# Dealing one burst of an attention kernel out over three units of its main loop

## The chip, the cores and the metric

The kernel runs on one core of one Trainium2 chip. The metric is the device time of one execution in microseconds (us). It is compared as a median over runs. Engines are named as in the profile: PE is the matrix engine (PEld its weight loads), DVE the vector engine, ACT the engine of the activations, POOL is GpSimd, SP the engine that only issues DMAs here.

## The reference

Attention whose scores are masked by a hash of six sign bits, and then a feed-forward stage with the maximum of three projections:

```python
def _attn_ref(q, k, v, proj):              # q, k, v: 4 x 8 heads x 768 x 64; proj: 64 x 6
    ...
    q_bits = (np.einsum('bhsd,dk->bhsk', q, proj) > 0).astype(np.int64)
    k_bits = (np.einsum('bhsd,dk->bhsk', k, proj) > 0).astype(np.int64)
    q_bucket = np.sum(q_bits * powers, axis=-1)
    k_bucket = np.sum(k_bits * powers, axis=-1)
    mask = q_bucket[:, :, :, None] == k_bucket[:, :, None, :]
    scores = scale * np.matmul(q, k.transpose(0, 1, 3, 2))
    scores = np.where(mask, scores, -1000000000.0)
    ...
    attn = np.exp(scores)
    attn = attn / (np.sum(attn, axis=-1, keepdims=True) + 1e-09)
    return np.matmul(attn, v).astype(np.float32)

def _moe_ref(x, w1, w2, w3, w_out):        # x: 3072 x 512; w1, w2, w3: 512 x 768; w_out: 768 x 512
    h = np.maximum(np.maximum(x @ w1, x @ w2), x @ w3)
    return (h @ w_out).astype(np.float32)
```

The output of the attention, with the heads side by side, is the `x` of the second function.

## The kernel before

**Units.** The main loop (L607 to L632) runs over 192 units, 48 to a batch (`UPB`). A unit is two blocks of 128 keys against 384 queries of one head: two score matmuls into one PSUM tile `sc` (L290, the sign bits ride along as extra rows of `S`), and one exponential on ACT (L292), which writes a weights tile `AT` of 128 x 768. There are 26 such tiles, used in turn. Six units make a group: the keys of two heads against one half of the queries.

**What a unit issues, in order.** Each engine works through its own queue in the order in which the program is written; no scheduler moves anything. A unit `u` issues: the scores of unit `u + 1` (before unit 35, of `u + 2`); whatever the table `at` holds for it (loads, `turn`, `narrow`, `place`); one piece of the feed-forward stage, if one is due (from unit 40 on, `ffn_at`); `gather(u)`; the entries of `firsts` for it; and, in some units, a `burst`.

**gather (L334 to L344).** From unit 36 on, DVE adds up the weights tiles of a group in `As` (L342, L344), so that fewer matmuls are needed for the sums. The first unit of three issues nothing.

**Values, sums, scaling (`quads`, L347 to L389).** Two groups make a quad. `values` (L317) runs 24 matmuls, 32 columns of the array each, four side by side, into a PSUM tile `av`; each quad needs two, w = 0 and w = 1. `sums` (L367) runs, for weights not added up before, another 24 matmuls of that kind into `sm`; then DVE makes the inverses: a transpose (`ys`, L326), an addition and a reciprocal (`rr`, L327 and L328). `scale` transposes the inverses back (`rb`, L374, once for both w), takes a small column (`sv`, L377) and writes one slice of `xT`, the input of the feed-forward stage (L386). The feed-forward matmuls of L405 read four slices of `xT` in turn, for the output piece `l`.

**Where the quads stand.** The first two quads of the first batch are dealt out by `quad_at`: sums, first values with their scaling, and second values with their scaling, each in a unit of its own (units 18, 20, 23 and 26, 29, 32). The third quad, groups 4 and 5, is a `burst` in unit 36: values, sums, values, and both scalings behind them. It fills the third and fourth slices of the first `xT`. In unit 40 the feed-forward stage begins to read that `xT`. The fourth quad of the batch is a burst in unit 48, and after that a burst of two quads comes every 24 units.

**PSUM.** From unit 34 on (`LAST`) the scores have two tiles `sc` (`s0`, `s1`), `av` has `m0`, and everything else takes `m1`, `m2`, `m3` in turn (L613).

**Inputs of the second batch.** `turn` (L197, DVE) transposes the loaded `nat` tile into `T32`, four pieces to a set. `narrow` (L202, POOL) turns that into bf16, `place` (L208, SP) moves it into `S` by DMA, and `quad_hash` (L218 on PE, L221 on DVE, L228 on SP) adds the sign bits. For one set the four turns stand in units 34 to 37.

Of the kernel before, what the change touches and what calls it, by code (L numbers as in the profile page):

```python
# [17 lines left out]
def kernel(  # L18
# [59 lines left out]
    def lay_out(**tags):  # L78
        rings.update(tags)
        if "pool" in rings:  # L80
            third.close()
        rings["pool"] = third.enter_context(tc.tile_pool(name="third_ps", bufs=1, space=bass.MemoryType.PSUM))
# [128 lines left out]
    def quad_hash(g):  # L211
        bp = ps_tile("bp")
        ts = [t32.pop((side, g)) for side in range(2)]
        for u in range(2):
            for side in range(2):
                for j in range(2):
                    r = 2 * side + j
                    nc.tensor.matmul(bp[Q * r : Q * (r + 1), 0:HALF], pj[:, u, :],  # L218
                                     ts[side][:, u, j * HALF : (j + 1) * HALF], start=(u == 0), stop=(u == 1))
        bits = b_pool.tile([P, HALF], BF16, tag="bits", name="bits")  # L220
        nc.vector.tensor_scalar(out=bits[:], in0=bp[:, 0:HALF], scalar1=0.0, scalar2=0.5,  # L221
                                op0=AluOp.is_gt, op1=AluOp.subtract)

        def send():
            for side in (1, 0):
                for j in range(2):
                    r = 2 * side + j
                    nc.sync.dma_start(s_of[side, g][D : D + KB, :, j * HALF : (j + 1) * HALF],  # L228
                                      bits[Q * r : Q * (r + 1), :])
        return send  # L230
# [34 lines left out]
    UPB = NU // B  # L265
# [3 lines left out]
    def unit_of(u):  # L269
        g, n = divmod(u, UPG)  # L270
        if g < 4:
            hd, n = divmod(u % (2 * UPG), UPG)
            return 2 * (g // 2) + n // MH, hd, n % MH
        return g, n // MH, n % MH
# [6 lines left out]
    def scores(u):  # L281
        g, hd, kp = unit_of(u)
        b, qh, jj = groups[g]
        hh = b * H + 2 * jj + hd
        (qn, qx), (kn, kx) = where[0, hh], where[1, hh]
        nb = NBITS if b == 0 else KB
        sc = ps_tile("sc", "sc")
        for j in range(2):
            m = 2 * kp + j
            nc.tensor.matmul(sc[:, j, 0:HALF], s_of[kn][0 : D + nb, kx, m * P : (m + 1) * P],  # L290
                             s_of[qn][0 : D + nb, qx, qh * HALF : (qh + 1) * HALF], start=True, stop=True)
        nc.scalar.activation(at_tiles[u % NAT][:, :, 0:HALF], sc[:, :, 0:HALF], ActFn.Exp,  # L292
                             bias=-SCALE * 0.25 * nb, scale=SCALE)
# [40 lines left out]
    def gather(u):  # L334
        g, hd, kp = unit_of(u)
        if u < 36 or kp == 0:
            return
        if kp == 1:
            as_of[g, hd] = as_pool.tile([P, 2, HALF], FP16, tag="as", name="As")
        t, new = as_of[g, hd], at_tiles[u % NAT][:, :, 0:HALF]  # L340
        old = at_tiles[(u - 1) % NAT][:, :, 0:HALF] if kp == 1 else t[:]
        nc.vector.tensor_tensor(out=t[:], in0=old, in1=new, op=AluOp.add)  # L342
        if kp == 2 and u >= 48:
            nc.vector.tensor_tensor(out=t[:, 0, :], in0=t[:, 0, :], in1=t[:, 1, :], op=AluOp.add)  # L344
# [103 lines left out]
    def when(u, f, *args):  # L448
        at.setdefault(u, []).append(lambda: f(*args))

    with tc.manual_schedule():
# [121 lines left out]
        def hash_due(u):  # L573
            if u in hash_at:
                when(u + 1, quad_hash(hash_at[u]))


        def burst(u, *gss):
            vals, sums, scale = quads(gss)
            every = [(i, w) for i in range(len(gss)) for w in range(2)]  # L580
            ahead = 2 if u == NU else 1
            for n, (i, w) in enumerate(every):
                if n == ahead:
                    sums()
                    hash_due(u)
                vals(i, w)
                if n == ahead:
                    for e in every[:ahead]:
                        scale(*e)
                if n >= ahead:  # L590
                    scale(i, w)


        firsts = {}

        def quad_at(gs, us, ua, ub):
            vals, sums, scale = quads([gs])
            for u, fs in ((us, [sums]), (ua, [lambda: vals(0, 0), lambda: scale(0, 0)]),
                          (ub, [lambda: vals(0, 1), lambda: scale(0, 1)])):
                firsts.setdefault(u, []).extend(fs)  # L600

        quad_at((0, 1), *[18, 20, 23])
        quad_at((2, 3), *[26, 29, 32])
        firsts.setdefault(32, []).append(lambda: hash_due(32))

        issued, MORE, LAST = 0, 11, 3 * UPB // 4
        for u in range(NU):  # L607
            while issued < min(u + 2 if MORE - 2 <= u < LAST - 1 else u + 1, NU - 1):
                issued += 1
                if issued == MORE:  # L610
                    lay_out(sc=['s2', 's0', 's1'], ms=['m0', 'm1'])
                if issued == LAST:
                    lay_out(sc=['s0', 's1'], ms=["m1", "m2", "m3"], av=["m0"])  # L613
                scores(issued)
            for f in at.pop(u, []):
                f()
            if u in ffn_at:
                ffn += ffn_groups(ffn_at[u])
            full = u % 24 == 23
            if full:  # L620
                gather(u)
            if ffn:
                ffn.pop(0)()
            if not full:
                gather(u)
            w = u - LAG
            for f in firsts.pop(u, []):
                f()
            if UPB // 2 <= w < UPB and w % 12 == 11:
                burst(u, [w // 6 - 1, w // 6])  # L630
            elif w >= UPB and w % 24 == 23:
                burst(u, [w // 6 - 3, w // 6 - 2], [w // 6 - 1, w // 6])  # L632
# [39 lines left out]
```

## Time and profile before

| what | value |
|---|---|
| median of 3 runs | 262.19 us (261.02 to 262.92) |
| profiled execution, its own time | 261.68 us |
| its span, first to last instruction | 259.9 us |
| PE busy | 252.7 us, 97% of the span |
| DVE busy | 208.1 us, 80% |
| ACT busy | 181.8 us, 70% |
| POOL busy | 78.0 us, 30% |
| PE's granted clock, mean | 0.998 |

The span is what the trace covers; the execution's own time is 1.78 us longer. Busy time is summed over the span and hides stages with other limits, so that the stretch of units 34 to 42, some 36 to 47 us into the span, has to be read by itself. Matmuls overlap each other: one is recorded with about 0.33 us, while the next follows after half of that.

### The profile page before, as it was taken

How to read it: one execution, taken by the hardware profiler on the slowest of the kernel's cores; microseconds unless marked ns; L12 is line 12 of the kernel's file. 1: busy time of each engine (PE TensorE's matmuls, PEld its weight loads, DVE VectorE, ACT ScalarE, POOL GpSimd, SP SyncE). 2: the span in 40 equal slices, each digit the busy share in tenths (PEclk: the TensorE clock that was granted, in tenths of full speed). 3: DMA queues.
4: the chain of work that ended last, by engine and by line, in shares of the span. 5: the costliest groups of instructions: out<-in, count | busy, mean ns of one | idle time of the engine just before them, and what ended most of it. 6: DMA issues, size and time to landing. Idle time of an engine off the chain costs nothing.

```text
span 259.9 us, 5896 instructions
## 1 busy us (share of the span) xinstructions
PE 252.7 (97%) x2207; PEld 139.8 (54%) x2207; DVE 208.1 (80%) x474; ACT 181.8 (70%) x276; POOL 78.0 (30%) x128
## 2 busy tenths in 40 slices
PE   8999998999999999999999999999999999999994
PEld 4455444555555555555555655555555555554552
DVE  2794988999989997999989998998758984884450
ACT  3989885939995499918995499918995589612322
POOL 4599921675616219131416216100000000000000
PEclk9999999999999999999999999999999999999999
DMA  6999997549992906660192906320120003000203
GB/s 212 376 239 128 183 255 207 167 131 207 175 262 63 195 6 149 215 188 15 47 257 59 200 3 120 122 68 14 42 81 3 0 3 121 3 0 32 93 0 121
DMA packets 22252, 30.92 MB, mean 119 GB/s; under 512 B 3057, under 2 KB 17745, under 8 KB 22225
## 3 DMA queue, kind: packets, MB, share of 16 engines
q0 software_dynamic: 9088, 12.59, 25.5%
q1 hardware_dynamic: 12848, 17.58, 21.2%
q8 instruction: 17, 0.28, 0.5%
q10 hardware_dynamic: 288, 0.39, 0.4%
q14 instruction: 11, 0.08, 0.1%
HBM read 25.17 MB, written 6.29 MB: 121 GB/s over the span
## 4 chain that ended last, share of the span: by engine, by line
PE 91%; DVE 6%; issue 1%; ACT 1%; DVEq 0%
PE l L405 36%; PE sc L290 22%; PE l L436 12%; PE av L317 10%; PE bp L218 3%; PE mp L132 2%; DVE xT L386 2%; PE bp L174 1%; DVE T L197 1%; DVE S L179 1%; PE wp L477 1%; PE sm L367 1%; PE bp L154 1%; ACT AT L292 1%; DVE rb L374 1%
## 5 line engine op out<-in xcount | busy, mean ns | idle before, releaser
L292 ACT ACTIVATE AT<-sc 128x768 f16<-128x768 f32 x192 | 152.5, 822 | 46.9 <-PE sc L290 40.6
L405 PE MATMUL l<-xT,w_sb 128*128 128x384 f16 x568 | 112.1, 325 | 0.0
L290 PE MATMUL sc<-S 72*128 72x384 bf16 (+1 forms) x384 | 91.6, 326 | 1.9 <-ACT AT L292 1.7
L405 PEld LDWEIGHTS <-w_sb 128*128 128x128 f16 x576 | 55.4, 97 | 39.2 <-DVE xT L386 1.2
L414 DVE TENSOR_TENSOR ht<-ht,l 128x384 f16<-128x384 f16 x95 | 52.1, 549 | 20.4 <-PE l L405 17.9
L290 PEld LDWEIGHTS <-S 72*128 72x128 bf16 (+1 forms) x384 | 36.3, 98 | 34.9 <-issue 9.3
L202 POOL TENSOR_SCALAR T<-T 128x768 bf16<-128x768 f32 x24 | 22.7, 944 | 80.2 <-DVE T L197 40.6
L436 PE MATMUL l<-wout_sb,ht 128*128 128x512 f16 x138 | 36.2, 378 | 0.0
L342 DVE TENSOR_TENSOR As<-As,AT 128x768 f16<-128x768 f16 x52 | 33.5, 645 | 2.2
L317 PE MATMUL av<-AT,vo 128*32 128x385 f16 x744 | 34.2, 327 | 0.2 <-DVE xT L386 0.2
L342 DVE TENSOR_TENSOR As<-AT,AT 128x768 f16<-128x768 f16 x52 | 30.1, 579 | 4.6 <-ACT AT L292 4.6
L412 ACT CAST ht<-l 128x384 f16<-128x384 f32 x47 | 22.4, 477 | 10.4 <-DVE ht L414 7.4
L317 PEld LDWEIGHTS <-vo 128*32 128x32 f16 x768 | 19.5, 96 | 15.1 <-issue 5.8
L197 DVE STREAM_TRANSPOSE T<-nat 128x384 f32<-128x384 f32 x48 | 26.5, 564 | 0.3
L386 DVE SCALAR_TENSOR_TENSOR xT<-av,sv,rb 128x384 f16<-128x384 f32 (+1 forms) x35 | 21.6, 617 | 1.2
L436 PEld LDWEIGHTS <-ht 128*128 128x128 f16 x138 | 13.3, 97 | 12.7 <-DVE ht L414 0.5
L344 DVE TENSOR_TENSOR As<-As 128x384 f16<-128x384 f16 x48 | 17.2, 358 | 1.7
L440 ACT COPY osb<-l 128x512 f32<-128x512 f32 x23 | 13.4, 582 | 6.7 <-PE l L436 6.7
L248 POOL DMA_DIRECT2D vo<-in_v_dram x24 | 13.3, 571 | 2.3 <-DMA wout_sb<-in_moe_w_out_dram 1.6
L143 POOL TENSOR_SCALAR S<-T 64x768 bf16<-64x768 f32 (+1 forms) x17 | 12.4, 730 | 4.3 <-DVE T L138 1.7
L179 DVE TENSOR_SCALAR S<-bp 6x384 bf16<-6x384 f32 x16 | 8.9, 555 | 2.7 <-PE bp L174 2.5
L374 DVE STREAM_TRANSPOSE rb<-rr 128x384 f32<-128x384 f32 x16 | 9.1, 569 | 0.1
(55 smaller groups left out, 116.9 us busy)
## 6 DMA issues: line engine op xcount, KB each, us to landing
out_dram<-osb SPq DMA_DIRECT2D x23, 256.0 KB
S<-T SPq DMA_DIRECT2D x48, 96.0 KB
nat<-in_k_dram POOLq DMA_DIRECT2D x16, 192.0 KB, 4.8
nat<-in_q_dram POOLq DMA_DIRECT2D x16, 192.0 KB, 5.3
w_sb<-in_moe_w_dram POOLq DMA_DIRECT2D x12, 192.0 KB, 4.3
vo<-in_v_dram POOLq DMA_DIRECT2D x24, 96.0 KB, 5.0
nat<-in_k_dram SPq DMA_DIRECT2D x10, 192.0 KB
nat<-in_q_dram SPq DMA_DIRECT2D x8, 192.0 KB
```

The lines of the kernel that those rows point to most:

```text
L197: nc.vector.transpose(t32[name][:, u, half * HALF : (half + 1) * HALF], i_)
L202: nc.gpsimd.tensor_scalar(out=t16[name][:, u, :], in0=t32[name][:, u, :], scalar1=RS, scalar2=1.0, op0=AluOp.mult, op1=AluOp.mult)
L290: nc.tensor.matmul(sc[:, j, 0:HALF], s_of[kn][0 : D + nb, kx, m * P : (m + 1) * P], s_of[qn][0 : D + nb, qx, qh * HALF : (qh + 1) * HALF], ...
L292: nc.scalar.activation(at_tiles[u % NAT][:, :, 0:HALF], sc[:, :, 0:HALF], ActFn.Exp, bias=-SCALE * 0.25 * nb, scale=SCALE)
L317: nc.tensor.matmul(av[r * Q : (r + 1) * Q, 0 : HALF + 1], vt[:, x, c + w : c + D : D // Q], at_of(g, m, hd)[:, 0 : HALF + 1], start=(m == ...
L342: nc.vector.tensor_tensor(out=t[:], in0=old, in1=new, op=AluOp.add)
L344: nc.vector.tensor_tensor(out=t[:, 0, :], in0=t[:, 0, :], in1=t[:, 1, :], op=AluOp.add)
L386: nc.vector.scalar_tensor_tensor(out=o, in0=av[p0:p1, 0:HALF], scalar=sv[p0:p1, :], in1=rc[p0:p1, :], op0=AluOp.add, op1=AluOp.mult)
L405: nc.tensor.matmul(ps[:, 0:HALF], w_sb[wi][:, jc, fb * P : (fb + 1) * P], xt[:, jc, :], start=(jc == 0), stop=(jc == NJC - 1))
L412: nc.scalar.copy(as_l(hts[fb]), l)
L414: nc.vector.tensor_tensor(out=as_l(hts[fb]), in0=as_l(hts[fb]), in1=l, op=AluOp.max)
L436: nc.tensor.matmul(ps[:, 0:DM], hts[fb][:, tb * P : (tb + 1) * P], wout_sb[:, fb, :], start=(fb == 0), stop=(fb == NFB - 1))
```

## The change

The third quad of the first batch is no longer a burst. It goes through `quad_at` like the first two: its sums stand in unit 36, its first values and their scaling in unit 37, its second values and their scaling in unit 38. So on PE the scores of units 38 and 39, which stood behind the burst, stand between its three parts, and the sums stand ahead of the values. On DVE the transpose `turn` of unit 37 and the addition of `gather(37)` stand between the parts of the quad instead of behind them. `quad_at` is rewritten so that sums may come in an earlier unit than, or the same unit as, the values. In a unit that holds entries of `firsts`, `gather` is issued behind them instead of ahead of them; before unit 36 `gather` issues nothing, so that this concerns units 37 and 38. The burst in unit 48 and all later ones are unchanged. On ACT, POOL and SP the order of instructions is the same as before.

```diff
         def quad_at(gs, us, ua, ub):
             vals, sums, scale = quads([gs])
-            for u, fs in ((us, [sums]), (ua, [lambda: vals(0, 0), lambda: scale(0, 0)]),
-                          (ub, [lambda: vals(0, 1), lambda: scale(0, 1)])):
-                firsts.setdefault(u, []).extend(fs)
+            for n, v in enumerate((ua, ub)):
+                firsts.setdefault(v, []).append(lambda n=n: vals(0, n))
+            firsts.setdefault(us, []).append(sums)
+            for n, v in enumerate((ua, ub)):
+                firsts.setdefault(max(v, us), []).append(lambda n=n: scale(0, n))
 
         quad_at((0, 1), *[18, 20, 23])
         quad_at((2, 3), *[26, 29, 32])
+        quad_at((4, 5), *[36, 37, 38])
...
-            if not full:
+            late = u in firsts
+            if not full and not late:
                 gather(u)
             w = u - LAG
             for f in firsts.pop(u, []):
                 f()
-            if UPB // 2 <= w < UPB and w % 12 == 11:
+            if late:
+                gather(u)
+            if w == UPB - 1:
                 burst(u, [w // 6 - 1, w // 6])
             elif w >= UPB and w % 24 == 23:
                 burst(u, [w // 6 - 3, w // 6 - 2], [w // 6 - 1, w // 6])
```

## The prediction

> **What bounds the kernel now.** I read the page first, for the engine that is full; then the busy times by stretch, for where it is not; then the timeline of PE, ACT and DVE around that place, one engine at a time.
>
> ```profile
> span 259.9 us, 5896 instructions
> ...
> PE 252.7 (97%) x2207; PEld 139.8 (54%) x2207; DVE 208.1 (80%) x474; ACT 181.8 (70%) x276; POOL 78.0 (30%) x128
> ```
>
> ```profile
> core 0: us, PE busy (x) PEld busy (x) DVE busy (x) ACT busy (x) POOL busy (x), PEclk, DMA share, GB/s
> ...
> 40.00:43.00 3.00, 3.00 (x73) 1.78 (x66) 2.11 (x6) 1.58 (x3) 0.00 (x0) 1.00 0.89 193
> 43.00:46.00 3.00, 1.83 (x10) 0.89 (x11) 2.90 (x8) 2.17 (x4) 1.16 (x2) 1.00 0.50 130
> 46.00:54.00 8.00, 8.00 (x51) 4.76 (x49) 7.79 (x16) 7.54 (x13) 4.30 (x7) 1.00 0.56 158
> ```
>
> PE is full nearly everywhere at a granted clock of 1.00. The stretch from 43 to 46 us is the exception: it holds 1.17 us without PE work, just behind the burst that the change takes apart. From 46 us to 225 us the trace shows PE waiting for nothing of weight. The most that this change can win is therefore about what lies idle here.
>
> PE in that place (columns: start, length, line, what, count, and in brackets the idle time before it):
>
> ```profile
> 38.77 1.15 PE L290 MATMUL sc<-S 70*128 70x384 bf16 x6
> 39.85 1.17 PE L317 MATMUL av<-AT,vo 128*32 128x385 f16 x24
> 40.84 1.15 PE L367 MATMUL sm<-AT,ones 128*32 128x384 f16 x24
> 41.82 1.16 PE L317 MATMUL av<-AT,vo 128*32 128x385 f16 x24
> 42.91 0.82 PE L290 MATMUL sc<-S 70*128 70x384 bf16 x4
> 44.69 0.48 PE L290 MATMUL sc<-S 70*128 70x384 bf16 x2 [0.96 <-ACT AT L292]
> 45.39 0.48 PE L290 MATMUL sc<-S 70*128 70x384 bf16 x2 [0.21 <-ACT AT L292]
> 45.71 0.81 PE L405 MATMUL l<-xT,w_sb 128*128 128x384 f16 x4
> ```
>
> The scores of unit 37 end the first row. Then the burst runs for 3.06 us without any scores. Behind it the scores of 38 and 39 fill the two `sc` tiles, and those of 40 and 41 wait for exponentials. Then the first feed-forward piece starts, at 45.71. ACT shows the other side:
>
> ```profile
> 39.36 2.22 ACT L292 ACTIVATE AT<-sc 128x768 f16<-128x768 f32 x3 [1.26 <-PE sc L290]
> 43.83 2.96 ACT L292 ACTIVATE AT<-sc 128x768 f16<-128x768 f32 x4 [2.25 <-PE sc L290]
> ```
>
> ACT starves for 2.25 us while PE runs the burst, and then PE starves while ACT catches up with four exponentials (38 to 41). DVE, from the waiting sums on:
>
> ```profile
> 39.73 1.50 DVE L197 STREAM_TRANSPOSE T<-nat 128x384 f32<-128x384 f32 x3
> 42.05 0.58 DVE L326 STREAM_TRANSPOSE ys<-sm 128x384 f32<-128x384 f32 x1 [0.82 <-PE sm L367]
> 42.66 0.17 DVE L327 TENSOR_SCALAR rr<-ys 128x12 f32<-128x12 f32 x1
> 42.87 0.23 DVE L328 RECIPROCAL rr<-rr 128x12 f32<-128x12 f32 x1
> 43.13 0.58 DVE L374 STREAM_TRANSPOSE rb<-rr 128x384 f32<-128x384 f32 x1
> 43.63 0.12 DVE L377 TENSOR_SCALAR sv<-av 128x1 f32<-128x1 f32 x1
> ...
> 44.51 0.62 DVE L386 SCALAR_TENSOR_TENSOR xT<-av,sv,rb 128x384 f16<-128x384 f32 x1
> 45.04 0.57 DVE L197 STREAM_TRANSPOSE T<-nat 128x384 f32<-128x384 f32 x1
> 45.53 0.52 DVE L342 TENSOR_TENSOR As<-AT,AT 128x768 f16<-128x768 f16 x1
> ```
>
> The last slice of `xT` is there at 45.13 (44.51 + 0.62). It was not what the first feed-forward piece waited for at 45.71: that was ACT, by way of the scores of unit 41.
>
> **The change on PE.** Nothing is added or removed: 72 narrow matmuls and the scores change places. From the rows: a group of 24 takes 0.99 (39.85 to 40.84), a pair of scores 0.33. A change between score matmuls and narrow ones costs 0.10 more: six scores from 38.77 would end their turn after 6 x 0.163 = 0.98, and the values follow after 1.08; the scores at 42.91 follow the values of 41.82 after 1.09 instead of 0.99. Between 39.85 and the first feed-forward matmul there was one such change; now there are five. With the sums starting at 39.85 (their PSUM tile was last read, at the latest, by the hash bits, which ended at 39.63), PE would do: sums 39.85, scores of 38 at 40.94, values 41.37, scores of 39 at 42.46, values 42.89, scores of 40 and 41 at 43.98 and 44.31, feed-forward at 44.64. That is 1.07 earlier than 45.71, with 0.40 paid for four more changes.
>
> [...] If every change waited for the recorded end of a 0.33 us matmul, it would cost 0.17 and not the 0.10 of the rows, the feed-forward piece would start at 44.99, and the gain on PE would be 0.72. [...]
>
> **Waits that this adds on PE.** In the new order values stand behind scores, and scores need a free `sc` tile. The scores of 38 need the exponential of 36 (over at 40.84), those of 39 that of 37 (41.58, 0.9 before they are due). ACT then goes on without its gap of 2.25: the exponential of 38 from 41.58 to 42.4, of 39 from 43.03 to 43.84, of 40 from 44.55, of 41 until 46.07, where it ended at 46.79 before. No score is held.
>
> **The change on DVE, which I expect to set the time.** The sums end at 41.0 instead of 41.99, so the wait of 0.82 goes: `ys` follows the three transposes at 41.2. By the start-to-start distances of the rows, `rr` stands at 41.8, the reciprocal at 42.0. But now the transpose of unit 37 comes here (42.3, 0.49 until the next start: 45.04 to 45.53), then `rb` at 42.8, `sv` at 43.3 (first values are done at 42.5), the first slice at 43.4. Next comes `gather(37)` at 43.95, whose weights have been there since 41.6. It holds DVE for 0.5 to 0.62 (its own 0.52; 0.62 to the dependent addition that followed it at 46.15). Then `sv` at 44.5, and the last slice from 44.7, done at 45.25 to 45.45. I take 45.35: 0.82 saved, some 1.05 put in front, so this slice comes 0.2 later than before, although sums stand first.
>
> The feed-forward piece reads that slice with its fourth matmul, which ran at 45.71 + 3 x 0.163 = 46.20. Its first three can run from 44.64; the fourth starts at about 45.35 + 0.05 = 45.40. So PE gains 0.80. The scores of 42 need the exponential of 40, over at 45.4, and follow at 45.56 where they stood at 46.36.
>
> **What is moved at no cost, and what covers it.** The additions behind the scaling: the `As` of unit 37 is used by the sums of unit 48, at 55.3 us, ten microseconds later. Without that cover the price would be the two additions, 1.1. The transpose of unit 37 comes 2.7 earlier, but POOL's `narrow` ahead of its own stands until 44.77 for a DMA, and a load issue at 45.67 follows, so POOL's next `narrow` stays at 46.34 and SP's `place` at 47.43; unit 60 needs that data, some 20 us later. On POOL and SP no queue order changes.
>
> **What is late next.** From unit 41 on everything moves 0.8 ahead. Scores of unit 48 (52.24) read hash bits issued on SP until 46.73, whose packets ended by about 48.6. The tightest date I found is `wout_sb`: issued by POOL at 56.26 and 57.00, landing after 8.3 to 9.5, so at the latest 65.8 and 66.5; first used at 67.15 and 68.13. With 1.3 in hand, 0.8 passes.
>
> **Sum.** 0.80 off the span: 259.9 becomes 259.1, and the profiled execution's 261.68 becomes 260.9. That execution lay 0.51 under the median, so the median goes from 262.19 to 261.4. Bounds: a gain of 0.4 if each DVE hand-over is somewhat slower than its row, 1.07 if PE alone sets it.
>
> **Rivals.**
> *DVE sets nothing, PE does.* If the last slice is ready by 45.1, the full 1.07 arrives: 261.1. For it speaks that independent DVE instructions started as little as 0.46 apart among the three transposes; against it the two instructions in front of the slice. [...]
> *The gain is given back later.* A date set by DMA, `wout_sb` first, holds PE where it held nothing before: 262.2. For it: its slack is only 1.3. Against it: POOL's issue there follows a `narrow` that waited 1.90 for DVE (at 53.50), and DVE moves along.
> *Slower: PE's queue is blocked by its own scores.* The second values stand behind the scores of 39, and these behind the exponential of 37. If ACT is late there, values, the last slice and the feed-forward stage go late together, where before values waited for no exponential beyond unit 35. The slice decides only past 46.14, so 0.8 later than computed; DVE reaches its `sv` 0.5 after the values end, and the scores have 0.9 in hand. So ACT must be 2.2 late, three exponentials of 0.74; every further one costs 0.74: 262.9. Nothing in the rows shows ACT that late, since it would start the stretch without a gap.
> That the change does not do what it says I leave out: the instruction order of both kernels shows the move.
>
> **How the numbers follow.** Forecast 0.58; PE alone 0.15; given back 0.17; slower 0.10. The likeliest is 261.4. The runs before spread from 1.17 under to 0.73 over their median, and a new median carries part of that. So the range runs from 260.1 (the 1.07, and 1.0 of spread) to 262.8 (nothing gained and 0.6 of spread, near the slower case). A bound of 1% (2.6 us), about what a measurement of this kernel can tell from no change, is over twice the idle time in the place. Only an effect far from it would reach that: faster 0.04, slower 0.05, within 0.91.
>
> **What would show it.** Right: no 2.25 gap on ACT between 41 and 44 us, PE without the idle 0.96, scores between three groups of 24, the first feed-forward matmuls at 44.6 with a short wait for `xT` before the fourth, the scores of 42 near 45.6, and the same 0.8 at unit 48 and at the end. Wrong in a step: `ys` later than 41.3, a change of tiling dearer than 0.10, or a wait for `sc` ahead of the second values. The prediction as a whole is wrong if the shift at 46 us is there and the end does not move, or if the first feed-forward piece ends later than 46.5.

## The result, and the profile after

The changed kernel takes 260.36 us (median of 8 runs, 260.04 to 261.07), the kernel before 262.36 us (8 runs beside them, 261.02 to 262.92): ratio 0.9929, 95% interval 0.991 to 0.9949. Its profiled execution took 260.33 us with a span of 258.6 us; before it was 261.68 and 259.9. A second set gave 260.28 against 261.92, ratio 0.9939 (0.9917 to 0.9961). So a change of 0.7% is told from none here; the prediction had put that limit at about 1%.

So the direction and the bound of 1% hold, but the gain is 1.6 to 2.0 us where 0.8 was forecast. The two traces show where a part of it lies. First the busy times by stretch of the changed kernel, columns as before:

```profile
40.00:43.00 3.00, 3.00 (x60) 1.27 (x55) 2.90 (x9) 2.33 (x4) 0.00 (x0) 1.00 0.91 168
43.00:46.00 3.00, 3.00 (x33) 1.48 (x26) 2.96 (x6) 2.28 (x4) 1.52 (x3) 1.00 0.40 103
```

PE is now full from 43 to 46 us, where it was busy for 1.83 of 3.00. The timeline of PE of the changed kernel, in the same place:

```profile
39.56 1.16 PE L367 MATMUL sm<-AT,ones 128*32 128x384 f16 x24
40.66 0.50 PE L290 MATMUL sc<-S 70*128 70x384 bf16 x2
41.08 1.17 PE L317 MATMUL av<-AT,vo 128*32 128x385 f16 x24
42.19 0.50 PE L290 MATMUL sc<-S 70*128 70x384 bf16 x2
42.62 1.17 PE L317 MATMUL av<-AT,vo 128*32 128x385 f16 x24
43.72 0.82 PE L290 MATMUL sc<-S 70*128 70x384 bf16 x4
44.38 0.81 PE L405 MATMUL l<-xT,w_sb 128*128 128x384 f16 x4
45.18 0.50 PE L290 MATMUL sc<-S 70*128 70x384 bf16 x2
```

Here this execution is 0.28 us ahead of the one before (its exponential of unit 36 starts at 39.79 instead of 40.07; that comes out of the first 8 us, below). From the start of the sums to the feed-forward piece it takes 4.82 us (39.56 to 44.38); before, from the start of the burst, it took 5.86 (39.85 to 45.71). No row has an idle time in brackets. ACT and DVE:

```profile
41.56 0.81 ACT L292 ACTIVATE AT<-sc 128x768 f16<-128x768 f32 x1 [0.26 <-ACT AT L292]
42.78 0.81 ACT L292 ACTIVATE AT<-sc 128x768 f16<-128x768 f32 x1 [0.41 <-PE sc L290]
44.31 1.51 ACT L292 ACTIVATE AT<-sc 128x768 f16<-128x768 f32 x2 [0.72 <-PE sc L290]
```

```profile
40.80 0.56 DVE L326 STREAM_TRANSPOSE ys<-sm 128x384 f32<-128x384 f32 x1
...
41.75 0.52 DVE L197 STREAM_TRANSPOSE T<-nat 128x384 f32<-128x384 f32 x1
42.19 0.53 DVE L374 STREAM_TRANSPOSE rb<-rr 128x384 f32<-128x384 f32 x1
...
44.03 0.62 DVE L386 SCALAR_TENSOR_TENSOR xT<-av,sv,rb 128x384 f16<-128x384 f32 x1
```

ACT's idle time of 2.25 in one piece has become 0.26, 0.41 and 0.72. DVE no longer waits for the sums, and the last slice of `xT` is done at 44.65, before the fourth feed-forward matmul (44.38 + 3 x 0.163 = 44.87) wants it.

A part of ACT's idle time before was not starvation. There the exponential of unit 38 starts 0.92 us behind its scores (42.91 to 43.83); in the changed kernel those of 39 and 40 start 0.59 behind theirs (42.19 to 42.78, 43.72 to 44.31). The trace of before has the wait for these scores over at 43.46, and the exponential starts 0.36 later; that of unit 40 in the changed kernel starts 0.05 behind its wait. The exponential of 38 starts late in all eleven profiles, 0.90 to 0.92 behind its scores. In the changed kernel that is the 0.26 at 41.56, and it holds nobody up, since the scores of 40 stand at 43.72 anyway. So by an estimate from these rows some 0.3 of what the change gains is this pause, which used to fall where PE waited for ACT; no run tests it by itself.

To compare runs without their different starts, I count from the start of the exponential of unit 36 to those of units 42 and 44 (from the timelines, one instruction at a time). What the kernels differ by at unit 44 they still differ by at unit 191, to 0.02 us.

| kernel | 36 to 42, us | 36 to 44, us |
|---|---|---|
| before | 6.97 | 8.78 |
| changed | 6.28 | 7.89 |
| before_again (clock halved for a while) | 7.31 | 10.43 |
| after_again | 6.28 | 7.89 |
| sums_first_only | 6.96 | 8.76 |
| sums_second | 6.91 | 8.77 |
| gather_ahead | 6.30 | 8.15 |
| values_together | 6.49 | 8.30 |
| turn_later | 6.28 | 7.89 |
| before_filled | 6.95 | 8.76 |
| before_more_idle | 9.01 | 12.85 |

The change is worth 0.89 us in this place. The profiled spans differ by 1.3: 0.29 is there before the first exponential already, and 0.15 appears at 237 us. The medians differ by 2.0. The experiments are about both: what makes the 0.89, and what the rest is.

### The profile page after: what moved, and what is told of

It reads as the page before. It is cut to its first block, busy times and chain, and to the rows that moved or that the text cites. A ratio compares the mean times of both kernels' runs of the same rounds, so it can differ in the third digit from the quotient of the medians.

```text
span 258.6 us, 5894 instructions
## 1 busy us (share of the span) xinstructions
PE 252.3 (98%) x2207; PEld 139.0 (54%) x2207; DVE 207.9 (80%) x474; ACT 182.0 (70%) x276; POOL 77.7 (30%) x128
## 4 chain that ended last, share of the span: by engine, by line
PE 91%; DVE 6%; issue 1%; ACT 0%; DVEq 0%
PE l L405 36%; PE sc L290 23%; PE l L436 12%; PE av L317 10%; PE bp L218 3%; PE mp L132 2%; DVE xT L386 2%; DVE T L197 1%; PE bp L174 1%; PE sm L367 1%; PE wp L477 1%; DVE S L179 1%; PE bp L154 1%; DVE rb L374 1%; PE l L425 1%
## 5 line engine op out<-in xcount | busy, mean ns | idle before, releaser
L414 DVE TENSOR_TENSOR ht<-ht,l 128x384 f16<-128x384 f16 x95 | 52.2, 550 | 20.6 <-PE l L405 17.9
```

What stands on the lines that cost most here:

```text
L414: nc.vector.tensor_tensor(out=as_l(hts[fb]), in0=as_l(hts[fb]), in1=l, op=AluOp.max)
```

## The experiments

**before_again and after_again: both kernels once more, unedited.**

> The kernel before, once more, against itself: a ratio of 1.000. What is open is why the medians lie 2.0 us apart (262.36 and 260.36) where the two traces put 0.89 us into units 36 to 42, 0.29 us into the first 8 us and 0.15 us behind 232 us. Theory A (the change itself is worth 0.9; the rest is the start, which is not the same in every run): this second profile has its exponential of unit 36 at another time than the 40.07 of the first, by up to 1 us, and from there to the end the same distances. Theory B (the change is worth 2 us in the main loop and the first profile of before was a lucky one): unit 36 stands at 40.1 again and the end is late by 1 us for other reasons.

> The changed kernel once more. By theory A its exponential of unit 40 stands 4.52 us behind that of unit 36 (before: 5.20), and that of unit 42 6.28 behind it (before: 6.97), as in the first profile, whatever the start does; the ratio to before lies between 0.992 and 0.997. By theory B the distances vary and the ratio is again 0.993 or less.

The kernel before against itself: ratio 1.0004 (0.9983 to 1.0025). The changed one: 0.9939, distances 6.28 and 7.89 as in its first profile, as theory A said. But before_again has a span of 261.5 with its start only 0.1 away from the first, so neither theory was right on it: the time is lost between units 41 and 44. Its busy times by stretch show how (the number behind POOL's is PE's granted clock):

```profile
45.00:46.00 1.00, 0.78 (x6) 0.46 (x5) 0.95 (x3) 1.00 (x3) 0.34 (x1) 1.00 0.31 84
46.00:47.00 1.00, 1.00 (x5) 0.47 (x4) 0.94 (x2) 0.97 (x2) 0.94 (x2) 0.54 0.14 44
47.00:48.00 1.00, 1.00 (x5) 0.46 (x4) 0.52 (x2) 0.89 (x2) 0.92 (x2) 0.50 0.08 28
48.00:49.00 1.00, 1.00 (x5) 0.50 (x4) 0.37 (x1) 0.09 (x1) 0.94 (x3) 0.50 0.76 219
49.00:50.00 1.00, 1.00 (x6) 0.56 (x5) 0.66 (x2) 0.80 (x1) 0.92 (x2) 0.75 0.43 62
```

The idle time ahead of it:

```profile
44.57 0.48 PE L290 MATMUL sc<-S 70*128 70x384 bf16 x2 [0.94 <-ACT AT L292]
45.27 0.48 PE L290 MATMUL sc<-S 70*128 70x384 bf16 x2 [0.22 <-ACT AT L292]
```

Just behind that idle time, from 46.08 to 49.50 us, PE runs at half its clock: the missing shares add up to 0.46 + 0.50 + 0.50 + 0.25 = 1.71 us, that is 3.42 us at half speed. 10.43 less 8.78 is 1.65 us of lost time. The mean granted clock of each run tells how often this happens: of the 69 runs of the kernel before in the sets from here on, 16 have a mean clock of 0.992 or 0.993 and a median of 263.0 us; the other 53 have 0.997 or more and a median of 261.6. Of 21 runs of the changed kernel and of turn_later (the same but for one transpose and the narrowing behind it) none is under 0.997. This is theory C of the next expectations; two runs test it.

**before_filled: PE kept busy in the idle time, nothing else.**

```diff
+        def fill(n):
+            fl = ps_tile("fl")
+            for _ in range(n):
+                nc.tensor.matmul(fl[:, 0:HALF], warm[:, 0:P], warm[:, :], start=True, stop=True)
+
+        when(38, fill, 5)
+        when(39, fill, 1)
```

> The kernel before, with six matmuls of the start-up kind (zeros by zeros into a spare PSUM tile that nobody reads) put where PE stands idle behind the burst: five ahead of the scores of unit 40, one ahead of those of 41. They add no wait, 6 x 0.163 us of work in 1.17 us of idle. Theory C (what the idle time costs beyond itself: in 7 of 35 runs of the kernel before the mean granted clock is 0.993 or less, and the profile of one of these shows PE at half its clock from 46.1 to 49.5 us, just behind the idle time, for 1.7 us of loss): with PE kept busy no run has a clock of 0.993 or less, the slow tail above 262.6 us is gone, and all else stays: unit 42 some 6.9 to 7.1 us behind unit 36, median 261.6 to 261.8. Rival (the half clock is not set off by the idle time): one run in five stays at 0.993 or less.

No run of 12 is under 0.998, where 7 of the 23 runs of before beside them are at 0.992 or 0.993. The longest times are gone (highest 262.2 against 263.36), and the distances stay at 6.95 and 8.76. Median 261.39 against 261.64, ratio 0.9976 (0.9956 to 0.9997). Work that computes nothing made the kernel a little faster, by an interval that ends just short of 1.

**before_more_idle: more idle time on PE.**

```diff
+        def hold():
+            for _ in range(2):
+                nc.scalar.copy(scrap[:], warm[:])
+
+        when(37, hold)
```

> The kernel before, with two copies on ACT (a zero tile into a tile that nobody reads, 0.48 us each) behind the exponential of unit 38. ACT comes 0.7 to 0.9 us later, and PE's idle time there grows from 1.2 to about 2 us. Theory C: most runs, not one in five, now have a clock of 0.993 or less, and the median lies 2.0 to 2.6 us above before (0.8 of ACT and 1.3 to 1.7 of half clock). Rival (chance, or another cause): one run in five, and a median 0.7 to 0.9 above before.

Nine of 12 runs have a clock of 0.993 or less, two 0.994, one 0.999. The median is 264.22 against 261.64, ratio 1.0083 (1.0059 to 1.0107): 2.6 us for 0.95 us on ACT. In the profiled run the clock stands at 0.50 in every stretch from 46 to 52 us, at 0.79 in the stretch of 1 us ahead and at 0.80 in the one behind. That makes 6.8 us, twice as long as in before_again. PE's rows there (line numbers are one higher in this kernel):

```profile
44.30 0.48 PE L291 MATMUL sc<-S 70*128 70x384 bf16 x2 [0.94 <-ACT AT L293]
45.95 0.80 PE L291 MATMUL sc<-S 70*128 70x384 bf16 x2 [1.17 <-ACT AT L293]
```

Filling the idle time took the half clock away (none of 12 runs has a mean clock of 0.993 or less, 7 of the 23 of before beside them have), widening it from 1.2 to 2.1 us made it nearly certain (11 of 12 at 0.994 or less). That PE's idle time sets it off is shown.

It does not do so each time: the profiled run of sums_first_only (next experiment) has the same gaps of 0.94 and 0.22 us and a mean clock of 1.00. So it stays open why the same idle time costs something in about one run of four (16 of 69) and nothing in the others.

**sums_first_only: the new order, but all in unit 36.**

```diff
-        quad_at((4, 5), *[36, 37, 38])
+        v45, sums45, scale45 = quads([(4, 5)])
+        firsts[36] = [sums45, lambda: v45(0, 0), lambda: v45(0, 1), lambda: scale45(0, 0), lambda: scale45(0, 1)]
```

> Only the order of the burst is changed: sums, values, values, both scalings, all in unit 36; nothing stands between them. Theory (dealing out brings the time, since ACT no longer starves): ACT is idle some 2.2 us during the burst as before, the scores of unit 41 wait for the exponential of 39, and unit 42 stands 6.9 to 7.0 us behind unit 36: no gain, ratio 0.999 to 1.001, though the last slice of xT is ready 0.8 us earlier than before. Rival (sums first brings it, by the earlier xT): unit 42 at 6.1 to 6.3, ratio 0.995 to 0.997.

Ratio 0.9993 (0.9977 to 1.0009), distances 6.96 and 8.76: no gain. DVE's last slice is done at 44.1 there, 1.2 us before the feed-forward piece starts, and PE still waits for ACT:

```profile
44.32 0.48 PE L290 MATMUL sc<-S 70*128 70x384 bf16 x2 [0.94 <-ACT AT L292]
```

**sums_second: dealt out, but in the old order.**

```diff
-        quad_at((4, 5), *[36, 37, 38])
+        quad_at((4, 5), *[37, 36, 38])
```

> The quad dealt out over the same three units, but in the order of before: first values in 36, sums and first scaling in 37, second values and second scaling in 38. PE's work and its five changes of tiling are the same. Theory (dealing out is what counts; sums first only gives DVE room): ACT and PE run as in the changed kernel until the feed-forward stage; the inverses come 1.5 us later, so that the last slice of xT is ready some 0.5 to 0.8 us later than in the changed kernel; its fourth matmul waits, and unit 42 comes at 6.6 to 6.9 behind unit 36 instead of 6.28. Rival (DVE has room for that too): 6.3.

PE starts the feed-forward piece 4.81 us behind the first values, as early as in the changed kernel, and then stands:

```profile
44.48 0.67 PE L405 MATMUL l<-xT,w_sb 128*128 128x384 f16 x3
46.01 0.32 PE L405 MATMUL l<-xT,w_sb 128*128 128x384 f16 x1 [0.86 <-DVE xT L386]
```

The distance to unit 42 is 6.91, just past the expected 6.6 to 6.9, and that to unit 44 is 8.77: the whole gain is gone. So neither half of the change brings anything alone. Dealing out takes ACT's wait away, sums first takes the wait for DVE away that would come in its place; the 0.89 needs both.

**gather_ahead: the additions of units 37 and 38 ahead of the scaling.**

```diff
-            late = u in firsts
+            late = False
```

> The changed kernel with the additions of gather in units 37 and 38 ahead of the scaling, as in other units. Theory (DVE had just enough room): the last slice of xT comes one addition, 0.5 us, later, at about 45.2 on the clock of the after profile instead of 44.65; the fourth matmul of the first feed-forward piece waits for it until 45.25 instead of 44.87, and the scores of unit 42 follow at 45.4 instead of 45.18: 0.2 of the 0.89 is lost. Rival (DVE already set the time, as the prediction had it): the whole 0.5 is lost. Third: nothing is lost, since the exponential of 40 sets the scores of 42 anyway.

```profile
45.10 0.32 PE L405 MATMUL l<-xT,w_sb 128*128 128x384 f16 x1 [0.27 <-DVE xT L386]
```

0.26 us is lost by unit 44 (8.15 against 7.89), as the first theory said. The place behind the scaling is worth 0.26 of the 0.89.

**turn_later: DVE relieved of one transpose.**

```diff
-                    when(t0 + dt * n2, turn, name, n2 // 2, n2 % 2)
+                    when(t0 + dt * n2 + 2 * (name == (1, 3) and n2 == 3), turn, name, n2 // 2, n2 % 2)
...
-                    when(t0 + dt * (1 + 2 * u2) + 1, narrow, name, u2)
+                    when(t0 + dt * (1 + 2 * u2) + 1 + 2 * (name == (1, 3) and u2 == 1), narrow, name, u2)
```

> The changed kernel with the transpose of unit 37, and the narrowing that follows it on POOL, two units later, so that DVE has one transpose (0.45 us) less between the inverses and the last slice of xT. Prediction's reading (DVE sets the time of the first feed-forward piece): unit 42 comes 0.4 us earlier, some 5.9 us behind unit 36 instead of 6.28. Theory (PE's own work, and behind it the exponential of 40, set it; DVE is done in time): unit 42 at 6.25 to 6.30, no gain, and the last slice still waits for the second values, which end at 43.8 on the clock of the after profile. The narrowing comes up to 1 us later, without effect. Theory C on the clock: no run at 0.993 or less.

6.28 and 7.89 to the hundredth, and 260.38 us: no gain. DVE now waits for PE ahead of the last slice:

```profile
43.70 0.16 DVE L377 TENSOR_SCALAR sv<-av 128x1 f32<-128x1 f32 x1 [0.24 <-PE av L317]
```

So in the changed kernel DVE does not set the time; it is in time by a little.

**values_together: both value groups in unit 37.**

```diff
-        quad_at((4, 5), *[36, 37, 38])
+        quad_at((4, 5), *[36, 37, 37])
```

> The changed kernel with both value groups and their scalings in unit 37, so that only three changes between score matmuls and narrow ones lie ahead of the feed-forward stage instead of five. If the changes of tiling were what counts (0.10 each), it gains 0.2 over the changed kernel: unit 42 stands 6.1 us behind unit 36 (changed kernel 6.28). Theory (ACT's supply counts): the scores of 39 come 1.0 us later, ACT idles again, the scores of 41 wait for the exponential of 39, and unit 42 comes at 6.6 to 6.8: half of the gain is lost.

6.49 and 8.30: 0.41 of the 0.89 is lost by unit 44. The two changes of tiling that are spared do not pay for ACT, whose idle time is 1.40 in one piece again, and PE waits 0.64 for it. The measured 6.49 lies under the expected 6.6 to 6.8, so a little less was lost than expected, but far from the 6.1 by which the changes of tiling alone would count.

## Why the prediction was right, and where it was not

*The idle time behind the burst as the source, and its size.* Right in the main: 1.17 us idle before, none after, and 0.89 gained where 0.80 was forecast. But it put the whole idle time down to the burst; by the estimate above some 0.3 of it was the late start of one exponential, which its own rows show (42.91 to 43.83).

*PE's sequence.* Right to 0.03 us: 4.82 from the sums to the feed-forward piece, 4.79 by the sum of rows. A change between score matmuls and narrow ones costs the 0.10 that was taken from the rows of before (in the changed kernel 40.66 to 41.08 is 0.42, for a pair of 0.33). The 0.17 each that a wait for a matmul's recorded end would have made is shown by no run.

*DVE sets the time.* Wrong. The forecast had the last slice 0.2 us later than before; it came at 44.65, or 44.93 on the clock of before, which is 0.2 earlier. The term that was mis-sized is the start-to-start distance of DVE instructions that need nothing from the one ahead of them. I took 0.48 to 0.62 from rows in which most did; in the changed kernel the reciprocal is followed after 0.15 instead of 0.26, the transpose of unit 37 after 0.44 instead of 0.49, and `gather(37)` after 0.51; `ys` also started 0.1 earlier than forecast, and all in all the slice came 0.4 ahead of the 45.35. turn_later shows that DVE was not the bound. What took the 0.15 between PE's 1.04 and the 0.89 is the exponential of 40: the scores of 42 stood 0.80 behind the start of the first feed-forward piece instead of 0.65, since ACT reached that exponential only at 44.31. The weight load for these scores shows the wait:

```profile
45.18 0.11 PEld L290 LDWEIGHTS <-S 70*128 70x128 bf16 x2 [0.37 <-ACT AT L292]
```

So the forecast of 0.80 was near for a wrong reason.

*The gather behind the scaling, at no cost.* Right, and it had a use (0.26).

*No date of a DMA takes the gain back.* Right: the differences of unit 44 still stand at unit 191, and the 0.15 at 237 us adds to the gain.

*The most that can be won is the idle time.* This is the step that failed. It left out that PE's clock can be halved behind the idle time, as in before_again for 3.42 us. In 16 of 69 runs that cost 1.4 us (263.0 against 261.6). The one profile of before that I had was not such a run: its clock was 1.00 there.

*How the 2.0 is made up.* 0.89 in the place; 0.15 at 237 us, which the profiles of both kernels show each time (below); and the runs with half clock, 16 of 69 at 1.4, about 0.3 in the mean. Together that is 1.35, where the means over all runs with a known clock differ by 1.6 (261.97 for the 69 of before, 260.38 for the 21 of the changed kernel and turn_later). Against before_filled, where no run has a mean clock under 0.998, the changed kernel is 1.0 to 1.1 faster (261.39 against 260.28 to 260.38), and 0.89 + 0.15 is 1.04. Against the 53 runs of before at 0.997 or more the means differ by 1.3, so some 0.2 is open there. The rest of the first comparison's 2.0 is open too, and half clock does not explain it: the shortest of the 16 runs took 262.76, and only two of that comparison's eight lie as high (262.78 and 262.92); the median of the other six is 262.19, still 1.8 above 260.36. The start may have a part in it: the first exponential comes from 0.73 us earlier to 0.35 later than in the first profile, over kernels that are the same up to there. So it is partly luck that the median of 260.36 lies within the range (260.1 to 262.8): the forecast gain accounts for less than half of the 2.0, and only the 1.0 that the range allowed for the spread of runs takes it down this far.

*The rivals.* PE alone would have given 1.07: it gave 1.04 to the first feed-forward matmul, and ACT took 0.15 back. The prediction had the exponential of 40 over at 45.4 (45.41 measured, on the clock of before), so by its own dates the scores of 42 could not have gained the 1.07. Given back later: did not happen. Blocked scores: no wait of a score appears ahead of the values.

## What to carry to other kernels

Where a burst on one engine starves a second, and then the first waits for the second to catch up, deal the burst out between the second's inputs; but look which result the burst owes to a third engine, and put that part first, or the wait only changes its name. On PE, a microsecond of idle time could cost more than itself here (in before_again 1.16 us idle, and 1.65 us lost behind it): count the runs by their granted clock before the size of an idle stretch is taken as the bound of a gain, since one profile may not show it. The price of interleaving tilings here was 0.10 us a change, 0.40 for the four more.

## What the runs showed of the hardware

- In the profile of before_again PE's clock was halved for 3.42 us behind only 1.16 us of idle time in two pieces (0.94 and 0.22). The mean clock that goes with it stands in 16 of 69 runs; with 2.1 us idle in 11 of 12 runs; with the idle time filled by matmuls on zeros in none of 12. sums_first_only, with the same two gaps, had it in one of 12 runs. What decides in a given run is open.
- Late in the kernel, two output copies on ACT stand 20.10 to 20.13 us apart in the profiles of before, before_again, before_filled, before_more_idle, sums_first_only and values_together, and 19.94 in those of the changed kernel, gather_ahead, sums_second and turn_later, with no change of work there. In before, one DVE addition (L414) starts 0.42 us behind the wait ahead of it instead of 0.06. The first six have 114 wait instructions in DVE's queue up to that point, the others 112. In the others a later addition, at 241 to 242 us, starts 0.4 late, behind 5.0 us of idle time of DVE. In all eleven profiles the late one has 575 recorded entries of DVE's queue (waits counted) ahead of it (in before it starts at 237.32 us, in the changed kernel at 241.36), and the late exponential of unit 38 has 63 of ACT's (43.83 and 41.56). So the pause goes with the position in the queue and not with the time; why was not tested.
